# Linear attention and a gated feed-forward layer on one core: the maxima of k pass through a DRAM row instead of a product

## The chip, the core and the metric

One NeuronCore of a Trainium2 chip runs the whole program. Its engines are TensorE (PE, matmuls; PEld is its weight load), VectorE (DVE), ScalarE (ACT), GpSimd (POOL) and SyncE (SP, which here issues every DMA). Each engine works through its own queue in order, and waits on semaphores of the others. The metric is the device time of one execution in microseconds (us); lower is better.

## What is computed

```python
q_s = softmax(q, axis=-1)              # q, k, v: (8 batches, 8 heads, 576, 64)
k_s = k - np.max(k, axis=2, keepdims=True)
k_s = np.exp(k_s)
k_s = k_s / (np.sum(k_s, axis=2, keepdims=True) + 1e-09)
kv  = np.einsum('bhsd,bhse->bhde', k_s, v)
x   = np.einsum('bhsd,bhde->bhse', q_s, kv)      # as (4608, 512): tokens x (head, dim)
xn  = x / sqrt(mean(x * x, axis=-1) + 1e-06) * rms_g
g, val = xn @ w_gate, xn @ w_val                 # (4608, 1536) each
out = (silu(g) * val) @ w_out                    # (4608, 512)
```

The weights come as 64-bit floats and are turned into 32-bit ones on the chip. The factor for the maximum of k differs for each head and each of its 64 columns, and cancels out of the quotient; it keeps the exponentials in range.

## The kernel before

**Tiles.** Heads go in pairs g = 0..3, so that a pair fills 128 partitions (2 heads x 64 columns). The 4608 tokens are cut into nine blocks j of 512, and d_ff = 1536 into twelve slices of 128; a step s = 12 j + i is slice i of block j, 108 in all. `f1(s, a)` (L839) is the first product for the gate (a = 0) or the value (a = 1), `f2(s)` (L878) the second. To keep accuracy on a faster format each 32-bit operand is split into a rounded high part and the rest (`w_hi`/`w_lo`, `o_hi`/`o_lo`, `h_hi`/`h_lo`), and three passes of four 128x512 matmuls replace one product: a block of 12 matmuls. In the first four steps `f2` is native instead: it multiplies the unsplit 32-bit tiles `gs` and `w`, which the profile shows as 8 matmul records.

**The k chain.** For batch b and pair g: `k_load` brings k in as 116 partitions x 2 heads x 5 rows x 64; `k_max` (L461, DVE) takes the maximum over the five rows, `k_tr` (L486, PE) transposes the result, `k_top` (L491, DVE) reduces it to one maximum for each of the 128 columns, a 128x1 tile `kx`. To subtract it the 128 numbers must lie along the free axis, the same on all partitions: `k_diag` (L333, ACT) puts them on a diagonal and `k_rows` (L500, PE) multiplies ones with that diagonal, which leaves the row on every partition in PSUM. `k_sub` (L506, DVE) subtracts it, `k_exp` (L510, ACT) follows, and `k_mm` (L518, PE) forms k'v and the sums in 20 small matmuls; `kv_hi`/`kv_lo` normalise. From batch 2 on `k_seg(m)` puts the products of three neighbouring pairs into one PSUM tile: `k_mm` of pair m-2, `k_rows` of pair m-1, `k_tr` of pair m. There are 24 such pairs.

**What sets the order.** `ORDER` is a list of some 2,800 step names, written by a planner, in which a suffix (:A, :D, :P) names the engine of a step that may run on several. The program is emitted in that order, so every engine's queue is the list cut down to its own steps. SP issues the DMAs in the list's order too, and stops at one whose buffer isn't free yet. The two PSUM tiles of `f1` (`ps_gv`) are freed by `g_mul` (L844) and `h_mul` (L851) on DVE. At the beginning, `conv_*` steps turn the weights into 32-bit numbers on ACT, DVE and POOL; the attention of blocks 0 and 1 has forms of its own (names with a 0). `n_sum`, `n_t`, `n_y0`, `n_y1`, `n_rows` (L767, L772 to L794) compute a block's root mean square, without which the block's first `g_mul` can't run.

Of the kernel before, what the change touches and what calls it, by code (L numbers as in the profile page):

```python
# [42 lines left out]
f1.0.1.1.2 f1.0.1.1.3 q_sum0.1.0 f1.0.0.2.0 f1.0.0.2.1 f1.0.0.2.2 w_hi.1.0.2:A n_y1.0 f1.0.0.2.3 f1.0.1.2.0 f1.0.1.2.1
f1.0.1.2.2 conv_low.1.2.1 w_lo.1.0:P f1.0.1.2.3 conv_low.3.0.2 conv_sign.0.2 w_lo.1.1:P n_rows.0 k_tr.1.0
conv_low.3.2.1 k_top.1.0 g_mul.0 conv_add.0.2.1 k_diag.1.0:A k_rows.1.0 n_cols.0 f1.1.0 silu.0 q_eps0.1.0 load_w.4.0
k_sub.1.0 load_w.4.1 v_ones.1.1 q_rec0.1.0 load_w.4.2 k_max.1.1 q_mul0.1.0:P conv_mul.2.0 v_load.1.1 conv_mul.2.1
h_mul.0 k_exp.1.0 conv_shift.2.0 f1.1.1 conv_shift.2.1 q_load0.1.3 conv_sign.2.0 conv_low.2.2.1 conv_sign.2.1
# [10 lines left out]
conv_sign.5.0 w_lo.4.1:P x_sq.1.0 x_lo.1.0 conv_mul.5.1 f1.4.0 conv_add.5.2.1 q_sum0.1.2 o_hi.4:A h_mul.3 conv_mul.6.0
o_lo.4:P conv_shift.5.1 conv_low.6.0.2 conv_shift.6.0 o_hi.5:A q_eps0.1.1 f1.4.1 conv_sign.5.1 conv_low.7.2.1 o_lo.5:P
q_rec0.1.1 g_mul.4 conv_mul.6.1 conv_sign.6.0 silu.4 q_mul0.1.1:P conv_shift.6.1 k_tr.1.1 conv_add.5.0.2 f2.3  # L60
q_load.2.0 k_top.1.1 conv_sign.6.1 k_diag.1.1:A conv_low.6.2.1 h_mul.4 conv_mul.6.2 h_hi.4:A conv_add.6.0.2
conv_shift.6.2 w_hi.5.0.2:A conv_sign.6.2 k_rows.1.1 warm.2.13 conv_low.8.0.2 load_w.10.0 k_sub.1.1 q_t0.1.1
load_w.10.1 k_max.1.3 load_w.10.2 w_lo.5.0:P f1.5.0 k_exp.1.1 q_c0.1.1:D w_lo.5.1:P q_max.2.0 w_hi.6.0.2:A q_half.2.0
h_lo.4:P k_mm.1.1 conv_mul.7.0 g_mul.5 f2.4 k_load.2.1 w_lo.6.0:P q_exp.1.3 k_eps.1.1 conv_shift.7.0 silu.5 k_rec.1.1
conv_sign.7.0 conv_add.6.2.1 kv_norm0.1.1:D q_sum0.1.3 conv_mul.7.1 f1.6.0 w_lo.6.1:P conv_mul.7.2 conv_shift.7.1
o_hi.6:A v_ones.1.3 q_eps0.1.2 conv_sign.7.1 v_load.1.3 conv_low.10.0.2 o_lo.6:P q_rec0.1.2 conv_shift.7.2 q_x0.1.1
conv_low.8.2.1 g_mul.6 q_mul0.1.2:P conv_low.10.2.1 conv_sign.7.2 f1.5.1 conv_add.7.0.2 x_hi.1.1:A q_load.2.1 x_sq.1.1
x_lo.1.1 silu.6 conv_mul.8.0 k_tr.1.2 f1.6.1 h_mul.5 x_acc.1.1:P kv_hi.1.1:A w_hi.7.0.2:A k_top.1.2 conv_shift.8.0
conv_add.7.2.1 k_diag.1.2:A h_hi.5:A conv_sign.8.0 kv_hi.1.0:A w_lo.7.0:P conv_mul.8.1 load_w.9.0 k_rows.1.2 h_mul.6
f1.7.0 load_w.9.1 k_sub.1.2 load_w.9.2 h_hi.6:A h_lo.5:P conv_shift.8.1 k_exp.1.2 q_max.2.1 h_lo.6:P conv_sign.8.1  # L70
q_t0.1.2 g_mul.7 w_lo.7.1:P f2.5 conv_mul.8.2 q_c0.1.2:D silu.7 conv_shift.8.2 conv_add.8.0.2 q_half.2.1 conv_mul.9.0
conv_sign.8.2 f1.7.1 o_hi.7:A conv_shift.9.0 conv_add.8.2.1 conv_mul.9.1 conv_sign.9.0 w_hi.8.0.2:A conv_shift.9.1
# [5 lines left out]
conv_mul.11.0 conv_mul.11.1 conv_shift.11.0 conv_add.10.0.2 conv_shift.11.1 f2.8 conv_sign.11.0 conv_sign.11.1
conv_mul.10.2 o_lo.9:P g_mul.9 w_hi.10.0.2:A conv_shift.10.2 silu.9 w_lo.10.0:P k_tr.1.3 f1.9.1 conv_sign.10.2
k_top.1.3 conv_mul.11.2 w_lo.10.1:P k_diag.1.3:A conv_shift.11.2 conv_add.11.0.2 conv_sign.11.2 k_rows.1.3 f1.10.0  # L80
k_sub.1.3 h_mul.9 k_exp.1.3 k_max.2.0 conv_add.10.2.1 f1.10.1 g_mul.10 conv_add.11.2.1 w_hi.11.0.2:A h_hi.9:A
q_eps0.1.3 v_ones.2.0 q_max2.2.0 q_rec0.1.3 w_lo.11.0:P v_load.2.0 o_hi.10:A silu.10 k_mm.1.3 q_mul0.1.3:P f1.11.0
# [857 lines left out]
```

## Time and profile before

| | |
|---|---|
| median of three runs | 1003.16 us (1001.92 to 1003.66) |
| the profiled execution, its own time | 1001.34 us |
| its span in the trace | 999.5 us |
| PE busy | 982.6 us (98%) |
| POOL / ACT / DVE busy | 738.0 / 612.5 / 468.8 us |
| chain that ended last: PE's share | 92% |

The busy time of an engine says how much work it has, not whether anybody waits for it. Matmul records overlap: a 128x512 matmul is recorded with some 0.39 us, while one follows the other every 0.227 us (12 in 2.72 us). So what a product costs is read from the starts of the rows around it, not from its own duration. A wait is shown in brackets behind the row that waited, with the engine and line that ended it.

### The profile page before, as it was taken

The page shows a single profiled execution, that of the slowest core. Times are in us where ns is not written, and L with a number is a line of the kernel's source. Part 1 is how long each engine was busy: PE and PEld are TensorE (multiplying, and loading weights), DVE is VectorE, ACT ScalarE, POOL GpSimd, SP SyncE. Part 2 cuts the span into 40 slices and gives each one's busy share as a digit, 9 for nine tenths or more (in the row PEclk, how much of TensorE's full clock was granted, in tenths as well). Part 3 has the DMA queues.
Part 4 walks back from the last instruction along what each step waited for, and adds up shares of the span by engine and source line. Part 5 has one row for each costly group of instructions (what it writes and reads, how often), then busy time and mean ns, then how long its engine had stood idle before and what let it go on. Part 6 is the DMA issues. An engine that isn't in the chain of part 4 may idle for free.

```text
span 999.5 us, 14416 instructions
## 1 busy us (share of the span) xinstructions
PE 982.6 (98%) x4897; PEld 797.1 (80%) x4897; DVE 468.8 (47%) x1135; ACT 612.5 (61%) x885; POOL 738.0 (74%) x643
## 2 busy tenths in 40 slices
PE   7899999999999999999999999999999999999998
PEld 5567887888888888888888888888888888888886
...
DMA packets 129687, 57.64 MB, mean 58 GB/s; under 512 B 101797, under 2 KB 123597, under 8 KB 129613
## 3 DMA queue, kind: packets, MB, share of 16 engines
...
q14 instruction: 36, 0.29, 0.1%
...
## 4 chain that ended last, share of the span: by engine, by line
PE 92%; DMA 3%; SPq 2%; DVE 2%; issue 0%; ACT 0%; POOL 0%; ACTq 0%; POOLq 0%; DVEq 0%
PE ps_gv L839 57%; PE ps_o L878 29%; PE ps_a L717 2%; PE ps_a L518 2%; DMA raw<-in_moe_w_out_dram 2%; DMA kt<-in_k_dram 1%; PE ps_a L500 1%; SPq L364 1%; DMA qt<-in_q_dram 0%; PE ps_a L646 0%; SPq L600 0%; PE ps_a L767 0%; SPq L450 0%; PE ps_a L486 0%; DVE cm L461 0%
## 5 line engine op out<-in xcount | busy, mean ns | idle before, releaser
L816 POOL TENSOR_TENSOR wl<-w,wh 128x512 fp32r<-128x512 f32 x216 | 278.7, 1297 | 103.9 <-ACT wh L328 102.3
L839 PE MATMUL ps_gv<-xh,wh 128*128 128x512 f32 x864 | 236.5, 395 | 2.9 <-ACT kt L510 1.7
L839 PE MATMUL ps_gv<-xl,wh 128*128 128x512 f32 x864 | 231.3, 390 | 0.0
L839 PE MATMUL ps_gv<-xh,wl 128*128 128x512 f32 x864 | 231.1, 389 | 0.0
L839 PEld LDWEIGHTS ps_gv<-xl,wh 128*128 128x128 f32 x864 | 162.2, 188 | 34.7 <-issue 0.2
L839 PEld LDWEIGHTS ps_gv<-xh,wl 128*128 128x128 f32 x864 | 162.1, 188 | 34.2
L839 PEld LDWEIGHTS ps_gv<-xh,wh 128*128 128x128 f32 x864 | 159.7, 188 | 37.1 <-ACT kt L510 2.1
L848 ACT ACTIVATE gs<-gs 128x512 f32<-128x512 f32 x108 | 68.3, 632 | 164.5 <-DVE gs L844 164.0
L844 DVE TENSOR_TENSOR gs<-ps_gv,r 128x512 f32<-128x512 f32 x108 | 74.1, 686 | 192.1 <-PE ps_gv L839 168.8
L824 POOL TENSOR_TENSOR ol<-w,oh 128x512 fp32r<-128x512 f32 x104 | 135.1, 1299 | 37.7 <-ACT oh L328 37.7
L860 POOL TENSOR_TENSOR hl<-gs,hh 128x512 fp32r<-128x512 f32 x104 | 134.7, 1296 | 29.5 <-ACT hh L328 29.5
L851 DVE TENSOR_TENSOR gs<-ps_gv,gs 128x512 f32<-128x512 f32 x108 | 74.5, 690 | 144.1 <-PE ps_gv L839 123.8
L328 ACT CAST wh<-w 128x1024 fp32r<-128x1024 f32 x108 | 113.1, 1047 | 29.2 <-PE ps_gv L839 28.2
L328 ACT CAST oh<-w 128x512 fp32r<-128x512 f32 x104 | 64.3, 618 | 83.3 <-PE ps_o L878 83.3
L878 PE MATMUL ps_o<-oh,hh 128*128 128x512 f32 x416 | 114.0, 394 | 0.0
L878 PE MATMUL ps_o<-oh,hl 128*128 128x512 f32 x416 | 112.0, 390 | 0.0
L878 PE MATMUL ps_o<-ol,hh 128*128 128x512 f32 x416 | 111.9, 389 | 0.0
L878 PEld LDWEIGHTS ps_o<-oh,hl 128*128 128x128 f32 x416 | 78.1, 188 | 16.7 <-POOL hl L860 0.2
L878 PEld LDWEIGHTS ps_o<-ol,hh 128*128 128x128 f32 x416 | 78.1, 188 | 16.6
L328 ACT CAST hh<-gs 128x512 fp32r<-128x512 f32 x104 | 64.4, 619 | 43.2 <-DVE gs L851 42.0
L878 PEld LDWEIGHTS ps_o<-oh,hh 128*128 128x128 f32 x416 | 76.8, 188 | 15.3 <-issue 0.4
L848 ACT ACT_TABLE_LOAD x43 | 55.2, 1283 | 0.8
...
## 6 DMA issues: line engine op xcount, KB each, us to landing
...
```

Of the source, the lines that this page charges most:

```text
L328: (e.copy if e is nc.scalar else e.tensor_copy)(dst, src)
L364: nc.sync.dma_start(t.rearrange("p (c f) -> p c f", c=NKT), src)
L518: nc.tensor.matmul(ps[h * D:(h + 1) * D, :D + 1], lhsT=ke[:n, h, j], rhs=vt[:n, j, h], start=(j == 0), stop=(j == len(rows) - 1))
L717: nc.tensor.matmul(px[:, c0:c1], lhsT=wt, rhs=mv[:, c0:c1], start=(i == 0), stop=(i == 2))
L816: on(nc.gpsimd).tensor_tensor(out=wl[:, a], in0=W(s % NF, a), in1=wh[:, a].bitcast(F32), op=ALU.subtract)
L824: on(nc.vector).tensor_tensor(out=ol, in0=W(s % NF, 2), in1=wo_[s][0].bitcast(F32), op=ALU.subtract)
L839: nc.tensor.matmul(pd[s], lhsT=m[:, a, c * P:(c + 1) * P], rhs=X[j, c][x], start=(n == 1), stop=(n == 3 * NKT))
L844: nc.vector.tensor_tensor(out=gs, in0=g_[s], in1=r_[s // NF], op=ALU.mult)
L848: nc.scalar.activation(g_[s], g_[s], AF.Silu)
L851: nc.vector.tensor_tensor(out=g_[s], in0=v_[s], in1=g_[s], op=ALU.mult)
L860: on(nc.gpsimd).tensor_tensor(out=hl, in0=g_[s], in1=h_[s][0].bitcast(F32), op=ALU.subtract)
L878: nc.tensor.matmul(po[t], lhsT=a[:, t * P:(t + 1) * P], rhs=w, start=(i == 0 and n == 0), stop=(i == NF - 1 and n == len(terms) - 1))
```

## The change

From batch 2 on `k_diag` and `k_rows` are gone. Two new steps on SP take their place: `k_put` writes the 128x1 tile of maxima to 128 numbers in DRAM, and `k_get` reads them back as one row for each of 116 partitions. `k_sub` reads that row from SBUF; 21 of its 24 runs go to POOL, which can't read PSUM and so couldn't do them before. The pool tag `cm` has three buffers instead of two, and `k_get` takes one of them. Steps 2 and 3 have split second products like those that follow, so two native ones (steps 0 and 1) are left. The order is planned anew from the first instruction on, with a late landing of the new DMAs: 45 steps of the first stretch move from POOL to DVE, 19 from ACT to DVE, and the loads at the beginning stand in another order.

```diff
+    dram = ctx.enter_context(tc.tile_pool(name="dram", bufs=4, space=bass.MemoryType.DRAM))
...
-        cm = ap.tile([P, P], F32, name="cm")[:KP if b else P0].rearrange("p (h d) -> p h d", h=2)
+        cm = ap.tile([P, P], F32, name="cm", bufs=3)[:KP if b else P0].rearrange("p (h d) -> p h d", h=2)
...
         if m >= 2:
             k_mm(*at(m - 2), t)
-        if 0 < m <= NG * (B - 2):
-            k_rows(*at(m - 1), t)
         if m < NG * (B - 2):
-            k_tr(*at(m), t[:, 2 * P:])
+            k_tr(*at(m), t[:, P:])
...
+    def k_put(b, g):
+        row_[b, g] = dram.tile([P, 1], F32, name="row")
+        nc.sync.dma_start(row_[b, g], kx_[b, g])
+
+    def k_get(b, g):
+        mb = ap.tile([P, P], F32, name="cm", bufs=3)[:KP]
+        nc.sync.dma_start(mb, row_[b, g].rearrange("p o -> o p").broadcast_to([KP, P]))
+        mb_[b, g] = mb.rearrange("p (h d) -> p h d", h=2)
...
-silu.60 q_lo.6.1:P k_seg.18 h_mul.60 w_hi.62.0.2:A h_hi.60:A f2.59 w_lo.62.0:P k_eps.6.0 k_load.6.3 k_top.6.2
-k_rec.6.0 k_diag.6.2:A k_sub.6.1 kv_hi.6.0:A h_lo.60:P k_exp.6.1 kv_lo.6.0 w_lo.62.1:P q_x.6.0 store.4.0:A f1.61.0
```

On PE, one `k_seg` in the middle of the program. Before, between two blocks, it has `k_mm` (L518), `k_rows` (L500) and `k_tr` (L486):

```order
L878 MATMUL ps_o<-oh,hl 128x512 x4
L518 MATMUL ps_a<-vt,kt 64x65 x10
L500 MATMUL ps_a<-cm,ones 116x128
L486 MATMUL ps_a<-ident,cm 128x116
L839 MATMUL ps_gv<-xh,wh 128x512 x4
```

Now (L849 and L888 are `f1` and `f2`, L528 is `k_mm`, L487 `k_tr`):

```order
L849 MATMUL ps_gv<-xh,wl 128x512 x4
L528 MATMUL ps_a<-vt,kt 64x65 x10
L487 MATMUL ps_a<-ident,cm 128x116
L888 MATMUL ps_o<-oh,hh 128x512 x4
L888 MATMUL ps_o<-ol,hh 128x512 x4
```

The product with ones has left the queue; what stands on either side is the same kind of block as before.

On DVE, the end of the root mean square of block 1, with `n_rows` (`r`), and the first `g_mul` that needs it. Before, `k_max` (L461) and `k_sub` (L506) stand between the two:

```order
L491 TENSOR_REDUCE kx<-ps_a 128x1
L794 STREAM_TRANSPOSE r<-y 128x512
L461 TENSOR_REDUCE cm<-kt 116x128
L506 TENSOR_TENSOR kt<-kt,ps_a 116x640
L688 RECIPROCAL sm<-sm 128x16
L844 TENSOR_TENSOR gs<-ps_gv,r 128x512
L801 TENSOR_REDUCE yt<-y 32x4 x4
```

Now (L804 is `n_rows`, L854 `g_mul`, L464 `k_max`, L861 `h_mul`):

```order
L676 TENSOR_TENSOR st<-st,sw 128x16
L804 STREAM_TRANSPOSE r<-y 128x512
L854 TENSOR_TENSOR gs<-ps_gv,r 128x512
L668 TENSOR_REDUCE sw<-sm 32x16 x4
L464 TENSOR_REDUCE cm<-kt 116x128
L861 TENSOR_TENSOR gs<-ps_gv,gs 128x512
```

`g_mul` stands right behind `n_rows`, and `k_max` behind `g_mul`; `k_sub` has gone further down. On PE three blocks (both `f1` of step 12 and `f2` of step 11) stand between `n_sum` of that block and the `f1` that needs this `g_mul`, where it was two and a `k_seg`.

On SP, one turn in the middle of the program. Before, the loads of k (`kt`), v (`vt`) and q (`qt`) and the stores (`out_dram`):

```order
L425 DMA kt<-in_k_dram 112x2x320
L425 DMA kt<-in_k_dram 3x2x320
L426 DMA kt<-in_k_dram 1x10x64
L450 DMA vt<-in_v_dram 112x5x64 x2
L450 DMA vt<-in_v_dram 3x5x64 x2
L452 DMA vt<-in_v_dram 1x2x64
L586 DMA qt<-in_q_dram 32x12x32 x4
L586 DMA qt<-in_q_dram 32x4x32 x4
```

Now `k_put` (L496) stands between the loads of k and v, and `k_get` (L500) behind the load of q:

```order
L496 DMA row<-kx 128x1
L453 DMA vt<-in_v_dram 112x5x64 x2
L453 DMA vt<-in_v_dram 3x5x64 x2
L455 DMA vt<-in_v_dram 1x2x64
L906 DMA out_dram<-ot 128x512 x2
L596 DMA qt<-in_q_dram 32x12x32 x4
L596 DMA qt<-in_q_dram 32x4x32 x4
L500 DMA cm<-row 116x128
```

From batch 4 on the list has three blocks of PE between a pair's `k_put` and its `k_get`, three or four between `k_get` and `k_sub`, and eleven or twelve more up to its `k_mm`. In batches 2 and 3 it is closer: for pair 2 of batch 2 `k_get`, `k_sub` and `k_mm` stand with one block between the first and the last.

## Rows read from the trace of the kernel before

**Rows 1.** The profile's page: busy time, share and instructions of each engine.

```profile
PE 982.6 (98%) x4897; PEld 797.1 (80%) x4897; DVE 468.8 (47%) x1135; ACT 612.5 (61%) x885; POOL 738.0 (74%) x643
```

**Rows 2.** Three of six stretches of the span. Columns: the stretch (us), its length, then busy time and, in brackets, instructions of PE, PEld, DVE, ACT and POOL, the granted clock of TensorE (1.00 is all of it), the DMA engines' share, GB/s.

```profile
30.00:63.00 33.00, 28.17 (x120) 18.36 (x119) 27.71 (x58) 27.34 (x36) 22.42 (x17) 1.00 0.80 243
63.00:175.00 112.00, 110.09 (x549) 85.78 (x546) 80.99 (x170) 92.80 (x140) 105.65 (x87) 1.00 0.47 134
...
275.00:725.00 450.00, 450.00 (x2318) 371.61 (x2317) 210.04 (x543) 287.69 (x411) 332.91 (x287) 1.00 0.19 44
```

**Rows 3.** The waits of PE over the whole span: the line that waited, what ended the wait, us in total, times, longest. The rows left out are waits in the first 33 us.

```profile
PE ps_gv L839 <- ACT kt L510: 1.7, 1, 1.7
PE ps_a L500 <- ACT cm L333: 1.7, 1, 1.7
...
PE ps_a L518 <- DVE w L385: 1.3, 1, 1.3
PE ps_gv L839 <- DVE gs L851: 1.2, 1, 1.2
...
PE ps_a L486 <- DVE y L790: 0.4, 1, 0.4
```

**Rows 4.** The timeline of PE around one `k_seg` with all three parts. Columns, here and in the other timelines: start, duration, engine, line, operation, tiles, shapes, number of records in the row, and in brackets a wait ahead of it.

```profile
311.15 1.07 PE L878 MATMUL ps_o<-oh,hl 128*128 128x512 f32 x4
...
312.89 0.47 PE L500 MATMUL ps_a<-cm,ones 128*116 128x128 f32 x2
313.20 0.26 PE L486 MATMUL ps_a<-ident,cm 116*128 116x116 f32 x1
...
314.24 1.08 PE L839 MATMUL ps_gv<-xl,wh 128*128 128x512 f32 x4
```

**Rows 5.** The timeline of PE around the `k_seg` without a transpose (739 to 742), and around the one that is `k_mm` alone (763 to 766).

```profile
739.12 1.07 PE L878 MATMUL ps_o<-oh,hl 128*128 128x512 f32 x4
...
740.85 0.47 PE L500 MATMUL ps_a<-cm,ones 128*116 128x128 f32 x2
...
742.09 1.07 PE L839 MATMUL ps_gv<-xl,wh 128*128 128x512 f32 x4
...
763.03 1.07 PE L839 MATMUL ps_gv<-xh,wl 128*128 128x512 f32 x4
...
765.80 0.39 PE L878 MATMUL ps_o<-ol,hh 128*128 128x512 f32 x1
```

**Rows 6.** The timeline of PE around a `k_rows` that stands alone between two groups of matmuls of `f1`.

```profile
128.76 1.08 PE L839 MATMUL ps_gv<-xh,wl 128*128 128x512 f32 x4
129.68 0.38 PE L500 MATMUL ps_a<-cm,ones 128*116 128x128 f32 x2
...
130.83 0.39 PE L839 MATMUL ps_gv<-xl,wh 128*128 128x512 f32 x1
```

**Rows 7.** The timeline of PE around a native `f2` (8 records), and further on around a split one (12).

```profile
48.06 3.59 PE L878 MATMUL ps_o<-w,gs 128*128 128x512 f32 x8
51.49 0.60 PE L633 MATMUL ps_a<-ident,xl 128*128 128x128 f32 x4
...
755.78 1.07 PE L878 MATMUL ps_o<-oh,hh 128*128 128x512 f32 x4
...
758.50 1.07 PE L839 MATMUL ps_gv<-xh,wh 128*128 128x512 f32 x4
```

**Rows 8.** The timeline of DVE at the end of the root mean square of block 1, and the row of PE that waits there.

```profile
156.24 0.70 DVE L794 STREAM_TRANSPOSE r<-y 128x512 f32<-128x512 f32 x1
156.87 1.28 DVE L461 TENSOR_REDUCE cm<-kt 116x128 f32<-116x640 f32 x1
...
158.96 0.62 DVE L844 TENSOR_TENSOR gs<-ps_gv,r 128x512 f32<-128x512 f32 x1
...
159.73 1.17 PE L839 MATMUL ps_gv<-xh,wh 128*128 128x512 f32 x4 [1.72 <-ACT kt L510]
```

**Rows 9.** The timeline of ACT ahead of the diagonal of the first pair of batch 1, and the `k_rows` of PE that waits for it.

```profile
39.70 0.68 ACT L371 ACTIVATE w<-w 128x512 int32<-128x512 uint32 x1 [0.43 <-DMA w<-in_moe_w_out_dram]
40.28 0.39 ACT L333 ACTIVATE cm<-ident,kx 128x128 f32<-128x128 f32 x1
...
40.72 0.48 PE L500 MATMUL ps_a<-cm,ones 128*116 128x128 f32 x2 [1.67 <-ACT cm L333]
```

**Rows 10.** The timelines of SP and DVE: the eight DMAs of one `q_load` and the last one of a `k_load`, then the `q_max` and the `k_max` that wait for them.

```profile
318.99 3.78 SPq L586 DMA_DIRECT2D qt<-in_q_dram  x8
...
337.68 0.68 SPq L426 DMA_DIRECT2D kt<-in_k_dram  x1
...
324.46 0.69 DVE L652 TENSOR_REDUCE st<-qt 128x16 f32<-128x512 f32 x1 [3.74 <-DMA qt<-in_q_dram]
...
340.11 1.32 DVE L461 TENSOR_REDUCE cm<-kt 116x128 f32<-116x640 f32 x1 [0.29 <-DMA kt<-in_k_dram]
```

**Rows 11.** Groups of instructions by line with their shapes: busy time and mean ns of one | idle time ahead of them. L816 is `w_lo`, L669 `q_sub`, L510 `k_exp`.

```profile
L816 POOL TENSOR_TENSOR wl<-w,wh 128x512 fp32r<-128x512 f32 x216 | 278.7, 1297 | 103.9 <-ACT wh L328 102.3 <-PE ps_a L767 1.6
...
L669 POOL TENSOR_TENSOR qt<-qt,st 128x512 f32<-128x512 f32 x28 | 29.4, 1053 | 18.5 <-DVE st L666 15.6 <-issue 2.2 <-POOL ol L824 0.3
...
L510 ACT ACTIVATE kt<-kt 116x640 f32<-116x640 f32 x28 | 20.7, 740 | 4.6 <-DVE kt L506 4.2
```

More of the change, by code (lines that the diff above doesn't have):

```diff
@@ L43 @@
[L43 to L47, printed above, removed]
@@ L58 @@
[L58 to L62, printed above, removed]
@@ L63 @@
[L63 to L72, printed above, removed]
@@ L78 @@
[L78 to L82, printed above, removed]
@@ new lines @@
+conv_add.10.0.2 o_hi.9:A v_load.2.0 h_lo.8:P load_w.11.0 k_rows.1.3 kv_hi.1.0:A w_hi.10.0.2:A conv_add.10.2.1
+w_lo.10.0:P q_t0.1.3 o_lo.9:P w_lo.10.1:P q_half.2.1 k_sub.1.3 load_w.11.1 q_load.2.2 load_w.11.2 x_acc.1.2:P
+conv_mul.11.0 k_max.2.0 k_exp.1.3 q_c0.1.3:D f2.8 h_mul.9 conv_shift.11.0 conv_mul.11.1 f1.10.0 conv_sign.11.0
+conv_shift.11.1 k_mm.1.3 conv_sign.11.1 g_mul.10 h_hi.9:A h_lo.9:D q_max.2.2 o_hi.10:A conv_low.11.0.2 conv_low.11.2.1
+conv_add.11.0.2 f1.10.1 k_eps.1.3 q_sub.2.0:P silu.10 q_half.2.2 k_rec.1.3 kv_norm0.1.3:A k_seg.0 k_top.2.0 h_mul.10
@@ new lines @@
+n_sum.2 q_max.3.3 silu.22 x_hi.2.3:A k_exp.3.0 k_put.3.1 x_lo.2.3 o_lo.20:D q_mul.3.1:D q_half.3.3 f1.23.0 o_hi.21:A
+h_hi.21:A h_mul.22 f1.23.1 k_seg.6 h_lo.20:P o_lo.21:P g_mul.23 n_t.2 f2.20 h_lo.21:P w_hi.24.0.2:A n_y0.2 n_y1.2
+w_hi.25.0.2:A w_lo.25.0:P q_rec.3.2 w_lo.24.1:P q_t.3.1 n_rows.2 k_eps.3.0 w_lo.24.0:P q_max2.3.3 k_get.3.1 v_ones.3.2
+q_sub.3.3:P f1.24.0 silu.23 h_hi.22:A q_hi.3.0:A h_mul.23 q_load.4.0 g_mul.24 k_rec.3.0 q_lo.3.0:P h_lo.22:P
+kv_hi.3.0:D k_top.3.2 f1.25.0 q_max.4.0 f2.21 f1.24.1 o_hi.22:A q_exp.3.3 o_lo.22:P q_mul.3.2:P k_sub.3.1:P k_load.3.3
@@ new lines @@
+x_lo.4.0 o_hi.37:A q_hi.4.2:A o_lo.37:P f1.37.1 g_mul.37 q_load.5.1 k_max.4.3 q_lo.4.2:P silu.37 f1.38.0 h_mul.37
+w_hi.39.0.2:A h_hi.37:A w_lo.39.0:P k_get.4.2 store.2.2:A h_lo.37:P f1.38.1 g_mul.38 store.2.3:A w_lo.39.1:P silu.38
+f2.36 h_mul.38 w_hi.40.0.2:A q_max.5.1 w_lo.40.0:P q_half.5.1 w_lo.40.1:P f1.39.0 o_hi.38:A h_hi.38:A o_lo.38:P
+h_lo.38:P f2.37 g_mul.39 k_sub.4.2:P silu.39 q_max2.5.1 k_exp.4.2 q_sub.5.1:P k_seg.11 f1.39.1 k_eps.4.1 k_load.5.0
+v_ones.4.3 k_top.4.3 o_hi.39:A k_rec.4.1 kv_hi.4.1:A o_lo.39:P q_exp.5.1 k_put.4.3 kv_lo.4.1 v_load.4.3 q_sum.5.1
@@ new lines @@
+k_sub.5.3:P q_exp.6.2 f2.52 h_mul.53 h_hi.53:A q_sum.6.2 w_hi.55.0.2:A h_lo.53:P q_half2.6.2 k_seg.16 k_exp.5.3
+w_lo.55.0:P o_hi.54:A f1.54.0 k_eps.5.2 k_load.6.1 k_top.6.0 k_rec.5.2 w_lo.55.1:P kv_hi.5.2:A kv_lo.5.2 k_put.6.0
+o_lo.54:P q_x.5.2 g_mul.54 v_ones.6.0 q_sum2.6.2 v_load.6.0 silu.54 f1.54.1 q_t.6.0 q_rec.6.2 q_mul.6.2:P x_hi.5.2:A
+q_load.6.3 x_sq.5.2 x_lo.5.2 f2.53 w_hi.56.0.2:A x_acc.5.2:P h_mul.54 k_max.6.1 h_hi.54:A w_lo.56.0:P f1.55.0
+o_hi.55:A h_lo.54:P k_get.6.0 w_lo.56.1:P o_lo.55:P f1.55.1 g_mul.55 silu.55 f2.54 h_mul.55 w_hi.57.0.2:A q_max.6.3
@@ new lines @@
+f1.63.0 o_hi.62:A h_hi.62:A o_lo.62:P h_lo.62:P f2.61 g_mul.63 k_sub.6.2:P silu.63 q_max2.7.1 k_exp.6.2 q_sub.7.1:P
+k_seg.19 f1.63.1 k_eps.6.1 k_load.7.0 v_ones.6.3 k_top.6.3 o_hi.63:A k_rec.6.1 kv_hi.6.1:A o_lo.63:P q_exp.7.1
+k_put.6.3 kv_lo.6.1 v_load.6.3 q_sum.7.1 q_x.6.1 w_hi.65.0.2:A h_mul.63 q_half2.7.1 f2.62 x_hi.6.1:A w_lo.65.0:P
+q_t.6.3 x_sq.6.1 x_lo.6.1 h_hi.63:A q_load.7.2 x_acc.6.1:P q_hi.6.3:A f1.64.0 h_lo.63:P o_hi.64:A k_max.7.0
+w_lo.65.1:P o_lo.64:P f1.64.1 g_mul.64 silu.64 q_lo.6.3:P k_get.6.3 q_sum2.7.1 q_rec.7.1 f2.63 h_mul.64 w_hi.66.0.2:A
```

468 lines of the change are left out of this document (236 added, 232 removed).

## The prediction

> **What bounds the kernel now.** I read the page's shares first, then the span cut into stretches, then PE's waits, then the timelines where PE waits or works off the products that go. The shares say PE 98%, POOL 74% [rows 1], an average over unlike stretches. The stretches settle it: from 275 to 725 us PE is busy for 450.00 of 450 us, and from 63 to 175 for 110.09 of 112; only from 30 to 63 us is it short, 28.17 of 33 [rows 2]. The granted clock is 1.00 in all of them, so no time is to be had from it. After 33 us PE waits in five places only: 0.4, 1.7, 1.2 and 1.3 us before 63 us, and 1.7 us later [rows 3]. So the time is a head of some 63 us, set by loads and by the conversion of the weights, and behind it the plain sum of PE's work. What leaves PE's queue behind the head shortens the run in full, as long as no other engine comes late.
>
> **The product with ones.** What it costs is read from the starts around it. A block of 12 matmuls takes 2.72 us (755.78 to 758.50) [rows 7], 0.227 us each. Around a full `k_seg` the starts run from 311.15 to 314.24 [rows 4]: 3.09 us, less eight matmuls of 0.227 (1.81) leaves 1.28 us. Without a transpose it is 742.09 - 739.12 - 1.81 = 1.16, and for `k_mm` alone 765.80 - 763.03 - 1.81 = 0.96 [rows 5]. So the transpose costs 0.12 and the product 0.20; the sum of a record's 0.47 us [rows 4] would be too much, since records overlap. A product that stands alone costs 130.83 - 128.76 - 1.81 = 0.26 [rows 6]. The 24 that go stand in `k_seg`s, so I take 0.20: 24 x 0.20 = 4.8 us, and 24 x 0.26 = 6.2 as the bound. No less than 4.8, for PE has no idle time there that could swallow it [rows 2].
>
> **The second products.** A native one takes 51.49 - 48.06 = 3.43 us, a split one 2.72 [rows 7]. Two are changed: 2 x 0.71 = 1.4 us less on PE. It adds four casts on ACT, three subtractions on POOL at 1.30 [rows 11] and one on DVE, between 63 and 90 us. POOL, which does 105.65 us of work in 112 there [rows 2], would have no room for 3.9 us more; what makes room is the list, which takes 45 steps off POOL in the first stretch. I count them at nothing. If that cover were missing, PE would wait up to 3.9 us.
>
> **The wait at 158 us.** `n_rows` ends at 156.94, but `g_mul` starts at 158.96, since `k_max` and `k_sub` stand between them on DVE; the next `f1` has no free PSUM tile and starts at 159.73, after 1.72 us [rows 8]. The label names ACT's `k_exp`; I put it down to `g_mul`, because the `f1` that starts there writes the tile that `g_mul` read, and both end within 0.1 us. In the new list `g_mul` follows `n_rows` at once, and three blocks of PE (8.2 us) instead of two cover the chain. I take all of it as gone: 1.7 us; bounds 0 and 1.7.
>
> **The head.** The waits of 0.4, 1.7, 1.2 and 1.3 us [rows 3] sum to 4.6 us. The largest shows their kind: the diagonal is at 40.28 behind a conversion that waited for its load until 39.70, and `k_rows` starts at 40.72 [rows 9]. The new list puts that `k_rows` amid the matmuls of step 0, and has all loads, conversions and `f1` pieces of the head in another order, so each of the four places is gone as such; but the amount of work up to each step is nearly the same, and new places will come. The trace can't show them. Bounds: all 4.6 gone, or 4.6 more. I take half as gained, 2.3, because the late part of the old waits came from ACT working off conversions in an unlucky order, not from a lack of bytes.
>
> **The DMAs that come in.** Every DMA here is issued by SP. Eight of a `q_load` take 3.78 us to issue, and `q_max` runs 1.69 us after the last (322.77 to 324.46); a `k_load` ends its issue at 338.36 and `k_max` runs at 340.11, 1.75 us later [rows 10]. So `k_put` and `k_get` take about 0.68 + 1.75 each, 4.9 us for the trip. From batch 4 on the list leaves 8.2 us (three blocks) from one to the other, as much again to `k_sub`, and some 30 us to `k_mm`. SP spends 48 x 0.68 = 33 us more on issuing, which delays nobody. Behind a waiting `k_put` stand the loads of v, stores and a load of q; `k_put` waits for `k_top`, which follows the `k_seg` that also frees v's buffer, so it holds them back by little, and v is used two `k_seg`s later. Behind `k_get` stands the next load of k. Cost: 0.
>
> **k_sub on POOL** has no row. A broadcast operand costs 1.053 us for 512 columns, two full ones 1.297 [rows 11]; for 640 columns that is 1.32 to 1.62. I take 1.6, two full reads being nearer. 21 of them are 34 us, against 45 steps at 1.0 to 1.3 that leave POOL. Late in the program only the addition remains: about 17 x 1.6 = 27 us on top of 332.91 in 450 [rows 2], 80%. That hides behind PE. The Trainium skill speaks against it: GPSIMD Engine Reference, section Key points, says that GpSimd shares its SBUF interfaces with VectorE and contends with DVE instructions that have two SBUF inputs, which the moved `w_lo`, `h_lo` and `o_lo` on DVE now are. No row here shows that pair at work; if contention doubled all 21, POOL would be at 86% there, still hidden. ACT loses 24 diagonals, which nobody waits for.
>
> **Sum.** From the profiled execution's 1001.34 us: -4.8 -1.4 -1.7 -2.3 = -10.2, so 991.1. The median of the runs stands 1.82 higher, at 1003.16; on that scale **993.0**.
>
> **Rivals.** *The head gives nothing back* (B): new places wait as long as the old ones did, the 1.7 us included. For it: the same bytes and conversions must come first, and DVE's share grows. Against it: POOL's load up to 175 us falls. Only the products and native steps count: 1003.16 - 6.2 = 997.0.
> *What PE saves is waited off* (D), so that the change doesn't do what it says: the new head has twice the old waits (4.6 + 1.7 = 6.3 us more), by splits that come before POOL is free. 1003.16 - 6.2 + 6.3 = 1003.3, no change.
> *The row comes late* (C), slower: in batches 2 and 3, eight pairs, the list is close. For pair 2 of batch 2 one block (2.7 us) stands between `k_get` and `k_mm`, but issue, landing, `k_sub` and `k_exp` need 0.68 + 1.75 + 1.6 + 0.74 [rows 10, 11] = 4.8, so PE is 2.1 us short unless SP runs ahead of the list, as it may. A POOL that waits in `k_sub` holds up `w_lo` and `h_lo` behind it as well. From six such pairs on (12.6 us) the gain is gone by more than can be measured: 1005.6, and with all eight (16.8) 1009.8; middle 1007.7. For it: SP's queue is in order and also holds stores that wait for PE. Against it: only one or two pairs are that close. The Trainium skill, DMA: Bandwidth & Descriptors, section Specifications, adds a reason: below 512 bytes a transfer does read-modify-write, and `k_put` writes 128 pieces of 4 bytes. No run here shows a write so small; a trip made longer by it would tighten all eight pairs.
>
> **How the numbers follow.** A 0.50 (993.0), B 0.26 (997.0), D 0.12 (1003.3), C 0.12 (1007.7). The low end takes every gain at its bound: 6.2 + 1.4 + 1.7 + 4.6 = 13.9, 989.3, so 989. The high end leaves out C and the upper half of D: 1001.5. A measurement of this kernel can tell some 0.2% (2 us) from no change; faster than 1001.2 is all of A and B, within 1001.2 to 1005.2 is D, above is C: 0.76, 0.12, 0.12.
>
> **What would show it.** A `k_seg` of 1.28 - 0.20 = 1.08 us between its neighbours; PE without waits from 63 us on, none at the first `g_mul` of block 1; the waits between 30 and 63 us summing to some 2 us; `k_sub` on POOL near 1.6 us. I am wrong if PE shows waits at `k_mm` in batches 2 and 3 that end with `k_exp` (C), or if the first `f1` of step 5 comes as late as before or later (B, D). If the product's place still costs time with the product gone, the first term fails.

## The result and the profile after

The changed kernel takes 1012.5 us (median of four runs, 1010.8 to 1013.9) against 1002.5 of the kernel before beside it: ratio 1.0097, 95% interval 1.0079 to 1.0116. It is 10 us slower where the prediction had 10 us less. The profiled execution took 1012.48 us, its span is 1010.7.

The page's shares, to be read against [rows 1]:

```profile
PE 981.8 (97%) x4857; PEld 797.4 (79%) x4857; DVE 516.7 (51%) x1178; ACT 564.5 (56%) x825; POOL 728.2 (72%) x622
```

PE's busy time is the same as before, within 1 us. That is no sign that the products still cost something: part of the new run goes at half the clock (0.50, rows below), where the same work counts for more. The span cut into stretches shows it (columns as in [rows 2]):

```profile
30.00:63.00 33.00, 32.21 (x140) 22.23 (x140) 30.32 (x64) 31.25 (x44) 28.56 (x27) 1.00 0.89 256
63.00:175.00 112.00, 112.00 (x568) 90.94 (x567) 94.80 (x189) 85.29 (x126) 91.74 (x72) 1.00 0.50 126
175.00:225.00 50.00, 44.46 (x224) 36.14 (x223) 34.88 (x78) 26.99 (x39) 27.79 (x22) 0.93 0.45 51
225.00:275.00 50.00, 47.87 (x240) 38.63 (x239) 41.18 (x94) 24.36 (x33) 29.79 (x24) 0.97 0.16 33
275.00:325.00 50.00, 41.36 (x211) 33.20 (x210) 26.88 (x65) 22.90 (x36) 24.45 (x21) 0.93 0.40 55
...
375.00:725.00 350.00, 349.55 (x1784) 287.33 (x1783) 162.97 (x418) 202.94 (x295) 281.52 (x238) 1.00 0.20 47
```

The head is better than before: 32.21 of 33 us busy against 28.17, then 112.00 of 112 against 110.09 [rows 2]. All is lost between 175 and 325 us, in batches 2 and 3. PE stands idle there for 5.54 + 2.13 + 8.64 = 16.3 us, and the granted clock, 1.00 before, is 0.93, 0.97 and 0.93. It is at its lower level, 0.50 (1.2 of 2.4 GHz), in three places:

```profile
181.95:188.70 6.75, 5.37 (x13) 4.40 (x14) 4.22 (x12) 2.83 (x5) 1.27 (x1) 0.50 0.22 50
229.75:233.10 3.35, 3.35 (x9) 2.57 (x8) 3.21 (x6) 2.11 (x3) 1.24 (x2) 0.50 0.45 112
294.60:301.30 6.70, 3.14 (x7) 2.51 (x8) 1.30 (x4) 0.00 (x0) 2.95 (x3) 0.50 0.90 69
```

PE works there for 5.37 + 3.35 + 3.14 = 11.9 us. At 1.00 that work takes about half as long (four matmuls of `f1` 0.91 us from start to start at 403.72, and 1.70 at 184.14), so the clock costs some 6 us on top of the waits. From 325 us on PE is as good as gap-free.

The waits of PE behind 35 us, the four largest (columns as in [rows 3]):

```profile
PE ps_o L888 <- DVE ot L338: 6.9, 1, 6.9
PE ps_a L727 <- DVE kv_lo L570: 5.7, 2, 5.0
PE ps_gv L849 <- DVE gs L861: 2.5, 3, 1.7
PE ps_a L487 <- DVE cm L464: 1.2, 1, 1.2
```

None is at `k_mm` (L528), where the rival C looked for them. They are at `f2` behind a store's buffer, at `q_x` (L727) behind a load of q, at an `f1`, and at a transpose behind a load of k. DVE is named each time, but DVE had been waiting itself, and the chain of waits says for what. Here it is from 280 to 310 us (start, duration, what):

```profile
280.24 8.44 DMA row<-kx
...
288.73 4.96 DMA cm<-row
...
293.76 8.34 DMA out_dram<-ot
...
302.12 2.00 DMA qt<-in_q_dram
```

One `k_put` is under way for 8.4 us, the `k_get` behind it for 5.0, a store behind the next `k_put` for 8.3, and the load of q only then. SP's own waits from 128 us on name the same thing (us in total, times, longest):

```profile
SPq L596 <- DMA row<-kx: 62.8, 16, 6.6
...
SPq L500 <- DMA row<-kx: 30.3, 4, 8.7
```

L500 is `k_get`, which must wait for its row. L596 is `q_load`, which has nothing to do with the row. It waits because the semaphores of SP's DMAs are used in turn, eight of them, so that each DMA waits for the one eight places ahead. That stands in the instructions, here at the third `k_put` (the six DMAs left out use semaphores 3 to 7 and 0):

```
L496 DMA row_1927<-kx_1906 128x1 [waits DMAHW2_49,DVE_49]
...
L596 DMA qt_2008<-in_q_dram 32x6x32 [waits DMAHW1_49]
L596 DMA qt_2008<-in_q_dram 32x6x32 [waits DMAHW2_49]
```

The last line needs semaphore 2 again, and so the landing of the `k_put` at the top. The timeline of SP at that place, `k_put` and the 16 DMAs of two loads of q:

```profile
161.74 0.34 SPq L496 DMA_DIRECT2D row<-kx  x1
...
166.75 13.78 SPq L596 DMA_DIRECT2D qt<-in_q_dram  x16
```

Sixteen take 13.78 us to issue, where twice the eight of [rows 10] would be 7.56; PE's first long wait, 5.04 us at 183.33, is for that q.

### The profile page after: what moved, and what is told of

Read it like the earlier page. It is cut to its first block, busy times and chain, and to the rows that moved or that the text cites. A ratio compares the mean times of both kernels' runs of the same rounds, so it can differ in the third digit from the quotient of the medians.

```text
span 1010.7 us, 14306 instructions
## 1 busy us (share of the span) xinstructions
PE 981.8 (97%) x4857; PEld 797.4 (79%) x4857; DVE 516.7 (51%) x1178; ACT 564.5 (56%) x825; POOL 728.2 (72%) x622
## 4 chain that ended last, share of the span: by engine, by line
PE 86%; DMA 7%; DVE 3%; SPq 1%; issue 1%; ACT 1%; POOL 0%; DVEq 0%; POOLq 0%; ACTq 0%
PE ps_gv L849 52%; PE ps_o L888 27%; DMA out_dram<-ot 3%; DMA kt<-in_k_dram 2%; PE ps_a L727 2%; PE ps_a L528 2%; DMA qt<-in_q_dram 1%; DMA row<-kx 1%; PE ps_gv L398 1%; PE ps_a L487 1%; DMA cm<-row 0%; PE ps_a L656 0%; PE ps_a L777 0%; DVE sw L668 0%; DMA w<-in_k_dram 0%
## 5 line engine op out<-in xcount | busy, mean ns | idle before, releaser
L826 POOL TENSOR_TENSOR wl<-w,wh 128x512 fp32r<-128x512 f32 x202 | 263.2, 1310 | 120.9 <-ACT wh L331 111.8
L849 PE MATMUL ps_gv<-xh,wh 128*128 128x512 f32 x864 | 236.8, 395 | 2.8 <-DVE gs L861 2.5
L849 PE MATMUL ps_gv<-xl,wh 128*128 128x512 f32 x864 | 233.8, 392 | 0.0
L849 PE MATMUL ps_gv<-xh,wl 128*128 128x512 f32 x864 | 232.7, 391 | 0.0
L849 PEld LDWEIGHTS ps_gv<-xl,wh 128*128 128x128 f32 x864 | 163.3, 189 | 34.9
L849 PEld LDWEIGHTS ps_gv<-xh,wl 128*128 128x128 f32 x864 | 163.3, 189 | 34.5
L849 PEld LDWEIGHTS ps_gv<-xh,wh 128*128 128x128 f32 x864 | 160.9, 189 | 37.1 <-DVE gs L861 4.0
L854 DVE TENSOR_TENSOR gs<-ps_gv,r 128x512 f32<-128x512 f32 x108 | 74.5, 690 | 188.9 <-PE ps_gv L849 169.5
L870 POOL TENSOR_TENSOR hl<-gs,hh 128x512 fp32r<-128x512 f32 x95 | 124.3, 1308 | 30.7 <-ACT hh L331 22.5
L834 POOL TENSOR_TENSOR ol<-w,oh 128x512 fp32r<-128x512 f32 x99 | 129.3, 1306 | 23.3 <-ACT oh L331 22.6
L861 DVE TENSOR_TENSOR gs<-ps_gv,gs 128x512 f32<-128x512 f32 x108 | 74.4, 689 | 122.9 <-PE ps_gv L849 107.2
L888 PE MATMUL ps_o<-oh,hh 128*128 128x512 f32 x424 | 117.3, 396 | 7.1 <-DVE ot L338 6.9
L888 PE MATMUL ps_o<-ol,hh 128*128 128x512 f32 x424 | 115.0, 392 | 0.0
L888 PE MATMUL ps_o<-oh,hl 128*128 128x512 f32 x424 | 114.4, 391 | 0.0
L888 PEld LDWEIGHTS ps_o<-oh,hh 128*128 128x128 f32 x424 | 79.0, 190 | 24.1 <-DVE ot L338 7.3
L888 PEld LDWEIGHTS ps_o<-ol,hh 128*128 128x128 f32 x424 | 80.2, 189 | 17.0
L888 PEld LDWEIGHTS ps_o<-oh,hl 128*128 128x128 f32 x424 | 80.0, 189 | 17.1 <-POOL hl L870 0.2
L701 POOL TENSOR_TENSOR qt<-qt,sm 128x512 f32<-128x512 f32 x26 | 28.0, 1077 | 27.9 <-DVE sm L698 27.1
```

What stands on the lines that cost most here:

```text
L701: on(nc.vector).tensor_tensor(out=qt_[j, g], in0=qt_[j, g], in1=sm_[j, g].unsqueeze(2).broadcast_to([P, M, 32]), op=ALU.mult)
L826: on(nc.gpsimd).tensor_tensor(out=wl[:, a], in0=W(s % NF, a), in1=wh[:, a].bitcast(F32), op=ALU.subtract)
L834: on(nc.vector).tensor_tensor(out=ol, in0=W(s % NF, 2), in1=wo_[s][0].bitcast(F32), op=ALU.subtract)
L849: nc.tensor.matmul(pd[s], lhsT=m[:, a, c * P:(c + 1) * P], rhs=X[j, c][x], start=(n == 1), stop=(n == 3 * NKT))
L854: nc.vector.tensor_tensor(out=gs, in0=g_[s], in1=r_[s // NF], op=ALU.mult)
L861: nc.vector.tensor_tensor(out=g_[s], in0=v_[s], in1=g_[s], op=ALU.mult)
```

## The experiments

Theory 1: `k_put` lands late, and what SP issues behind it comes late with it. Theory 2: the new order of batches 2 and 3 is at fault, whatever carries the maxima. Theory 3: the read by 116 partitions is at fault. All times in one paragraph are of kernels that ran on one chip unless said otherwise; there the kernel before took 1001.8 to 1002.1 us.

**e1_landing: small DMAs alone.** For each form:

```diff
+            f()                                           # one put, or one read of a row
+            nc.vector.tensor_scalar_add(src, src, 0.0)    # waits for its landing
```

> This kernel leaves out the whole computation: it issues one small DMA at a time, four times each, and a DVE instruction that waits for its landing, then fills the output with zeros. Theory 1 (the 128 pieces of 4 bytes are slow to land by themselves): about 8 us from issue to the DVE instruction for the 128 pieces of 4 bytes that lie together, 2 to 2.5 us for 4 pieces of 128 bytes and for one of 512. Rival (k_put is late because the other loads of batches 2 and 3 are in the way): about 2 to 2.5 us for every form, since nothing else is in flight here. Theory 3 (the read is at fault): 4 us or more for the row read by 116 partitions, 2 us for the row read once.

Part of the timeline. L40 is the put of 128 pieces of 4 bytes side by side, L43 the same 64 bytes apart, L49 4 pieces of 128 bytes, L55 32 pieces of 4 bytes; L74 is DVE when the put has landed:

```profile
25.98 0.34 SPq L40 DMA_DIRECT2D a<-src  x1
...
33.09 0.23 DVE L74 TENSOR_SCALAR src<-src 128x128 f32<-128x128 f32 x1 [5.91 <-DMA a<-src]
33.34 0.34 SPq L43 DMA_DIRECT2D a<-src  x1
34.85 0.23 DVE L74 TENSOR_SCALAR src<-src 128x128 f32<-128x128 f32 x1 [1.53 <-DMA a<-src]
...
36.87 0.26 SPq L49 DMA_DIRECT2D a<-src  x1
38.08 0.23 DVE L74 TENSOR_SCALAR src<-src 128x128 f32<-128x128 f32 x1 [1.24 <-DMA a<-src]
...
39.76 0.31 SPq L55 DMA_DIRECT2D a<-src  x1
42.72 0.23 DVE L74 TENSOR_SCALAR src<-src 128x128 f32<-128x128 f32 x1 [3.00 <-DMA a<-src]
```

From issue to landing, 7.1 us side by side (33.09 - 25.98; 7.0 to 7.3 in three rounds, 9.6 for the first DMA of the run), 1.5 us when 64 bytes or 512 bytes apart (1.9 in the last round), 1.2 us as 4 pieces of 128 bytes or one of 512, 3.0 us for 32 pieces of 4 bytes side by side, and 1.4 us for 32 pieces of 16 bytes, which are as many bytes as the first form. So neither the number of pieces nor the bytes make it slow, but pieces of 4 bytes that are neighbours in DRAM: (7.1 - 1.5) / 128 = 44 ns for each, as an estimate, and (3.0 - 1.5) / 32 = 47 for the short form. The row read by 116 partitions took 2.7 us (22.78 to 25.45, with another put issued 0.46 us ahead of it) and the row read once 1.24. The rival falls, since next to nothing else was in flight: a read of 512 bytes, issued 0.27 us ahead of the put. Theory 3's 4 us for the read isn't met.

The slow put's time doesn't pass in the DMA engines' own packets. For 5.5 of its 7.1 us their share and their GB/s (the last two columns) are nil:

```profile
27.50:33.00 5.50, 0.00 (x0) 0.00 (x0) 1.00 0.00 0
```

**e2_fast_put: the maxima leave in 4 pieces of 128 bytes.**

```diff
+        kr = small.tile([P, 32], F32, name="kr")
+        nc.vector.transpose(kr, kx_[b, g].broadcast_to([P, 32]))
...
-        nc.sync.dma_start(row_[b, g], kx_[b, g])
+        nc.sync.dma_start(row_[b, g].rearrange("(a c) o -> a (c o)", c=32),
+                          kr.rearrange("(a r) c -> a r c", r=32)[:, 0])
```

> The kernel after, with one DVE transpose ahead of k_put, so that the maxima leave from 4 partitions as pieces of 128 bytes. Order, list and number of DMAs are the same. Theory 1: k_get no longer stands behind k_put for 8 us, SP's waits on row fall from 93 us to under 20, PE's waits between 175 and 325 us from 16 to under 4, time 990 to 997 us. Theory 2 (the new order of batches 2 and 3 is itself at fault: loads that stand too late in the list, steps moved to DVE): the waits stay, 1008 to 1013. Theory 3 (the read): the same, 1008 to 1013.

989.1 us, ratio 0.9879 (0.9860 to 0.9898): faster than both kernels, with the same list. PE's only wait behind 35 us, and SP's issue of the 16 DMAs that took 13.78 us above (two views):

```profile
PE ps_gv L852 <- DVE gs L864: 1.0, 3, 0.5
```

```profile
169.36 8.07 SPq L599 DMA_DIRECT2D qt<-in_q_dram  x16
```

The transpose costs DVE 0.20 us each. Theories 2 and 3 said 1008 or more, and fall as explanations of the loss.

**e3_fixed_row and e4_no_put: the wait of k_get taken away, then k_put as well.**

```diff
-        nc.sync.dma_start(mb, row_[b, g].rearrange("p o -> o p").broadcast_to([KP, P]))
+        nc.sync.dma_start(mb, fixed.rearrange("p o -> o p").broadcast_to([KP, P]))
```

and in e4 every `k_put` taken off the list.

> The kernel after, in which k_get reads a row of constants written once early, so the maxima are not subtracted but the number 4, which cancels out of the quotient; k_put is still issued, with no reader. So k_get never waits for k_put, but a k_put that lands late still holds up the eighth DMA behind it. Theory 1 with the direct wait as its main part: 990 to 997 us. Theory 1 with the turn of eight as its main part: 1000 to 1009, SP's waits at L596-like loads of q on row stay near 60 us. Theories 2 and 3: 1008 to 1013.

> As the kernel with the fixed row, but k_put is left out altogether; k_get stays, with its read by 116 partitions, the order too. Theory 1: 990 to 996 us, no wait of PE over 1.5 us between 175 and 325 us. Theory 2: 1008 to 1013. Theory 3: 1006 to 1013, since the read is as before.

e3: 1004.3 us, ratio 1.0019 (1.0003 to 1.0036). e4: 987.5 us, ratio 0.9863 (0.9847 to 0.9880). In e3 nobody needs the row, and still SP's loads of q wait for it:

```profile
SPq L632 <- DMA row<-kx: 39.2, 15, 3.7
```

So the price of `k_put` splits in two, by the ratios. From e4 to e3 (1.0019 - 0.9863) it is 15.6 us, for what `k_put` does to the DMAs behind it; from e3 to the changed kernel (1.0097 - 1.0019) 7.8 us, because `k_get` waits for it at the head of SP's queue; each of the two is known to some 2 us. The read with its 116 pieces, which e4 keeps, costs nothing that can be seen: e4 is the fastest of all.

**e5_spread_put: e3 with the pieces 64 bytes apart.**

```diff
-        row_[b, g] = dram.tile([P, 1], F32, name="row")
+        row_[b, g] = dram.tile([P, 16], F32, name="row")[:, :1]
```

> The kernel with the fixed row (it subtracts the number 4 in place of the maxima, and k_put has no reader), with one change: the 128 pieces of 4 bytes of k_put lie 64 bytes apart in DRAM and not side by side. Number, size and place of the pieces in the list stay. Theory 1, sharpened by the landing times alone (7.0 us side by side, 1.5 us when 64 bytes apart): the turn of eight is free again, 987 to 990 us, as without k_put. Rival, after the rule that a transfer under 512 bytes does read-modify-write: pieces of 4 bytes are dear wherever they lie, 1003 to 1006 us, as with the fixed row.

988.75 us, ratio 0.9876 (0.9858 to 0.9894), so the 15.6 us between e3 and e4 are gone although 128 pieces of 4 bytes are still written. It is the neighbourhood of the pieces, in the kernel as alone.

**e6_product_in_2_3: the product back in batches 2 and 3, the slow k_put from batch 4 on.**

```diff
+        if 0 < m <= 2 * NG:
+            k_rows(*at(m - 1), t)
         if m < NG * (B - 2):
-            k_tr(*at(m), t[:, P:])
+            k_tr(*at(m), t[:, 2 * P:])
```

> The kernel after, with the old product in batches 2 and 3 (k_diag behind k_top on ACT, k_rows in k_seg, k_sub on DVE) and the slow k_put from batch 4 on, 16 of 24. Theory 1: from batch 4 on the list has room for a landing of 7 to 8 us, so nothing is lost there, and 8 products cost 8 x 0.20 = 1.6 us more than the version with the fast put (989.1): 990 to 993 us. Theory 2 (the new order of batches 2 and 3 is at fault whatever carries the maxima): 1005 to 1013. If the slow landing costs time in every batch: 996 to 1005.

997.3 us, ratio 0.9957 (0.9942 to 0.9972). By its number this is the third case, but the trace speaks against that case. From the start of `g_mul` of step 28 to that of step 80, e6 takes 756.49 - 297.72 = 458.77 us, e2 with the fast put 458.21, the changed kernel 459.57 and the one before 462.76. So from batch 4 on the slow `k_put` costs 0.6 to 1.4 us in all. What e6 lacks against e2 was lost by step 28, beside 8 products (1.6 to 2 us) in two waits of PE that e2 hasn't, and 0.97 of the clock from 225 to 275 us (1.5):

```profile
PE ps_a L757 <- DVE xl L779: 2.7, 2, 2.5
PE ps_a L757 <- ACT acc L774: 1.9, 1, 1.9
```

The first ends with DVE, which works off a `g_mul`, a `w_lo` and that `xl` in a row; all eight `k_sub` of these batches are on DVE in e6, which may have pushed it there. The second I can't place. So 990 to 993 was too low for a reason of e6's own, and what e6 leaves of theory 2 is at most these two waits and the clock, some 6 us. That the slow `k_put` costs so little from batch 4 on fits the list: from `k_put` to `k_sub` it leaves six or seven blocks there, 16 us or more, and to `k_mm` eight to thirteen more (not the eleven or twelve said above).

**e7_put_by_pool and e12_put_by_act: k_put from other queues.**

```diff
-        nc.sync.dma_start(row_[b, g], kx_[b, g])
+        nc.gpsimd.dma_start(row_[b, g], kx_[b, g])      # e7; e12: nc.scalar
```

> The kernel after, with k_put issued by GpSimd and not by SP, so it has a queue and semaphores of its own and no longer takes a place in the turn of eight. It still lands late, and k_get still waits for it at the head of SP's queue. Theory 1, turn of eight as the larger part (1004.3 - 987.5 = 16.8 us by the fixed row and the kernel without k_put): 1012.5 - 16.8 = 995.7, 992 to 1000 us; SP's waits on row at the loads of q are gone, those at k_get stay at 30 us or more. If the direct wait is what matters: 1005 to 1013. If GpSimd pays more than about 2 us for each issue in batches 2 and 3, some us on top.

> The kernel after, with k_put issued by ACT and not by SP. It keeps its place in the turn of eight semaphores that SP's DMAs also go through, but leaves SP's queue. Reading 1 (the turn of eight alone): as after, 1008 to 1013 us, SP's loads of q wait on row as before. Reading 2 (place in SP's DMA queue): as with GpSimd's put, 992 to 998 us. Both: in between. ACT issues 24 DMAs more, 0.4 us each, and waits for kx there, which costs PE little.

e7: 993.8 us, ratio 0.9926 (0.9908 to 0.9944). e12, on another chip: 997.7 us, ratio 0.9952 (0.9934 to 0.9971); its rows are from the slowest of its four runs, 1002.4 us. SP's waits on the row, first e7, then e12:

```profile
SPq L500 <- DMA row<-kx: 36.4, 3, 15.6
```

```profile
SPq L596 <- DMA row<-kx: 45.6, 11, 7.3
SPq L500 <- DMA row<-kx: 38.6, 4, 17.5
```

With GpSimd's put the loads of q no longer wait on the row, only `k_get` does. With ACT's put SP still takes part in the same turn and waits 45.6 us at loads of q, yet 14.5 us of the loss are gone by the ratios (17.1 in e7; against e4, 8.9 us stay in e12 and 6.3 in e7). So the turn of eight alone, reading 1, doesn't carry the loss. One thing e7 and e12 have in common: SP no longer stands at `k_put` until `kx` is there, as it did for up to 11.1 us, with all loads behind it. By itself that costs nothing: in e5 SP stands there just as long, 19.3 us in three waits, 11.1 at most, as in the changed kernel. So why the two gain is not shown.

**e11_behind_a_put: a load and a store behind one put, nothing else in flight.**

```diff
+                put()                 # none, side by side, 64 bytes apart, 4 pieces, by ACT
+                load()
+                store(t % 36)
```

> This kernel leaves out the whole computation: three times it issues, with nothing else in flight, a load of 112 x 5 x 64 numbers and a store of 128 x 512, first alone, then behind a put of 128 pieces of 4 bytes side by side, behind one with the pieces 64 bytes apart, behind one of 4 pieces of 128 bytes, and behind the side-by-side put when ACT issues it; DVE waits for the load, ACT for the store, GpSimd for the put. Reading 1 (only SP's turn of eight is held up): load and store land as soon behind the slow put as alone, about 2 and 3 us after their issue. Reading 2 (what stands behind a slow put in the same DMA queue lands after it as well): load and store land 5 us or more later behind the side-by-side put, and as if alone behind the other two; with ACT's put as if alone if each engine has a queue of its own, late if the writes hold up the DMA engines or the memory themselves.

Three of the five forms, second round; L38 is the load, L70 DVE when it has landed, L45 the put, L57 ACT's put, L60 GpSimd when the put has landed:

```profile
40.08 0.32 SPq L38 DMA_DIRECT2D kt<-in_k_dram  x1
...
42.43 0.33 DVE L70 TENSOR_SCALAR kt<-kt 128x320 f32<-128x320 f32 x1 [2.37 <-DMA kt<-in_k_dram]
...
43.95 0.34 SPq L45 DMA_DIRECT2D row<-src  x1
44.38 0.38 SPq L38 DMA_DIRECT2D kt<-in_k_dram  x1
...
52.78 0.61 POOL L60 TENSOR_SCALAR src<-src 128x128 f32<-128x128 f32 x1 [14.68 <-DMA row<-src]
52.88 0.37 DVE L70 TENSOR_SCALAR kt<-kt 128x320 f32<-128x320 f32 x1 [8.82 <-DMA kt<-in_k_dram]
...
64.78 0.33 ACTq L57 DMA_DIRECT2D row<-src  x1
64.97 0.32 SPq L38 DMA_DIRECT2D kt<-in_k_dram  x1
...
73.37 0.38 DVE L70 TENSOR_SCALAR kt<-kt 128x320 f32<-128x320 f32 x1 [8.43 <-DMA kt<-in_k_dram]
```

Alone the load lands 2.35 us after its issue, behind the slow put after 8.50 (52.88 - 44.38), 0.1 us behind the put itself; in the third round it is 10.6, 2.2 us behind the put. The store takes 2.6 us alone and 10.5 behind it. Behind the other two forms both are within 0.6 us of alone. Behind ACT's put the load takes 8.4 to 9.6 us, so leaving SP's queue doesn't help what is issued right after. Reading 2 holds, in its stronger form. The Trainium skill has both halves of this: DMA: Bandwidth & Descriptors, section Issuing engines are not separate DMA queues, says that DMAs of all issuing engines run on the same 16 DMA engines, and its section Queues, rings and completion order says that a DMA's semaphore write lands only after every earlier write of that DMA engine, across queues. The rows of ACT's put agree.

**e8_before_no_product: the first term by itself.** The kernel before, its list without `k_diag` from batch 2 on, `k_sub` subtracting 4 there:

```diff
-        if 0 < m <= NG * (B - 2):
-            k_rows(*at(m - 1), t)
```

> The kernel before, in its own order, without k_diag and k_rows from batch 2 on; k_sub subtracts the number 4 from a constant tile in place of the maxima. This is the first term of the prediction by itself. By the working: 24 x 0.20 = 4.8 us less, ratio 0.9952 (997.3 on this scale), 6.2 at most. Rival (the product lies beside other work): no change, 1002.

998.0 us, ratio 0.9963 (0.9951 to 0.9975): 3.8 us less, 2.5 to 4.9. The starts of `g_mul` say more. Against the kernel before, e8 is 2.16 us late at step 14 (168.92, 166.76) and 3.20 early at step 80 (758.29, 761.49): 5.4 us for the 22 products between, 0.24 each, 5.9 for all 24. It came late to step 14 because its clock was down in two stretches where it was 1.00 before:

```profile
40.00:50.00 10.00, 8.85 (x30) 6.69 (x31) 9.93 (x21) 9.87 (x14) 5.68 (x6) 0.83 0.54 128
...
150.00:175.00 25.00, 23.06 (x114) 18.29 (x113) 19.04 (x53) 17.79 (x25) 19.38 (x21) 0.93 0.28 77
```

**e9_fast_put_again and e10_native_f2: the second products.** e10 is e2 without `o_hi`, `o_lo`, `h_hi`, `h_lo` of steps 2 and 3:

```diff
-o_hi.2:A h_hi.2:A o_hi.3:A o_lo.2:P h_lo.2:P o_lo.3:P h_hi.3:A h_lo.3:D
```

> The version with the fast put once more, beside the next kernel on the same chip, as the better version and as the base for the term of the second products. Theory 1: 987 to 991 us, ratio 0.986 to 0.990.

> The version with the fast put, with the second products of steps 2 and 3 native again (no o_hi, o_lo, h_hi, h_lo there), the list otherwise the same. By the term of the prediction 2 x 0.71 = 1.4 us slower than the version with split ones. Rival (the casts and subtractions that the split ones need on ACT, POOL and DVE cost PE more than they save): 1 us or more faster.

e9: 988.3 us, ratio 0.9869 (0.9852 to 0.9885). e10: 990.75 us, ratio 0.9890 (0.9875 to 0.9904). Native is 2.1 us slower by the ratios; the intervals overlap, so the sign fits the term of 1.4 us and the size is not settled.

## Why the prediction was wrong

The starts of `g_mul` in the five traces show where time was won and lost (us; a step is not quite the same work in the old order and the new):

| step | before | after | e2 | e4 | e8 |
|---|---|---|---|---|---|
| 12 | 158.96 | 149.60 | 151.99 | 149.18 | 159.79 |
| 28 | 298.73 | 313.10 | 293.09 | 289.65 | 299.52 |
| 40 | 405.50 | 419.36 | 398.78 | 395.40 | 405.19 |
| 80 | 761.49 | 772.67 | 751.30 | 747.91 | 758.29 |

The changed kernel is as early as e4 at step 12 (0.4 us apart) and 23.5 us later at step 28. PE's 16.3 us of waits and the 6 us of clock make 22.3 of these, so next to nothing else went wrong.

**The step that failed** is the one on the DMAs that come in: "about 0.68 + 1.75 each, 4.9 us for the trip", "which delays nobody", "it holds them back by little", "Cost: 0". The rows it was priced by were loads [rows 10]; a write of 128 neighbouring pieces has no such row. Alone it took 7.1 us and the read 2.7, in the kernel 8.4 and 5.0, so the trip is 9.8 to 13.4 us. And it delays others: a load issued behind it lands after it (8.5 us and not 2.35 in e11), and SP's loads of q wait for it in their turn (62.8 us). The cost was 23.4 us by the ratios of e4 and of the changed kernel (1.0097 - 0.9863), of which 7.8 through `k_get`'s own wait and 15.6 through the DMAs behind.

**Rival C** had the sign and the batches, but not the mechanism. It priced 2.1 us for each pair whose row is late at `k_mm`, 12.6 to 16.8 us. PE never waits at `k_mm`; the bill came through loads of q and k and through stores. That SP's queue is in order and also holds stores was named there as a point for it, and it deserved to be the mechanism. The Trainium skill's rule (DMA: Bandwidth & Descriptors, section Specifications) that a transfer below 512 bytes does read-modify-write pointed at the right instruction, but its condition, size alone, doesn't tell the slow write from the fast ones here: the same 4-byte pieces land in 1.5 us 64 bytes apart, and 128-byte pieces in 1.2 us.

**The products.** 4.8 us, bound 6.2: by e8 it is 5.9. In the trace of after a full `k_seg` reads so:

```profile
408.25 1.07 PE L888 MATMUL ps_o<-oh,hl 128*128 128x512 f32 x4
...
411.08 1.08 PE L849 MATMUL ps_gv<-xl,wh 128*128 128x512 f32 x4
```

411.08 - 408.25 - 1.81 = 1.02 us, where 1.08 was forecast and 1.28 stood before [rows 4]: a product cost 0.26, nearer to the bound (the one that stood alone) than to the 0.20 taken. The term is right, a little small.

**The wait at 158 us** is gone, with no wait of PE between 63 and 175 us. Right.

**The head** was put at 2.3 us, half of its waits. e4 has all of the change but `k_put`. By its ratio it gains 13.7 us; less 5.9 for products, 1.4 for `f2` and 1.7 for the wait that leaves 4.7, give or take 2. Two stretches of e4 show it directly (columns as in [rows 2]):

```profile
0.00:30.00 30.00, 22.49 (x165) 15.00 (x165) 23.11 (x57) 19.26 (x38) 15.04 (x36) 1.00 1.01 238
30.00:63.00 33.00, 32.51 (x142) 22.58 (x143) 30.18 (x64) 31.20 (x43) 28.88 (x28) 1.00 0.91 268
```

From 30 to 63 us PE idles 0.49 us where it was 4.83 [rows 2]; up to 30 us it works 22.49 us where it was 23.67, so 1.2 us of the 4.3 were paid there. The head gave 3 to 5 us: mis-sized, on the side of caution.

**The second products**: the sign stands, 1.4 us lies within what e9 and e10 leave open.

**k_sub on POOL** was taken at 1.6 us, hidden:

```profile
L516 POOL TENSOR_TENSOR kt<-kt,cm 116x640 f32<-116x640 f32 x21 | 33.9, 1614 | 0.0
```

1614 ns, and POOL's `w_lo` went from 1297 ns [rows 11] to 1310. Right. The contention that the Trainium skill warns of (GPSIMD Engine Reference, section Key points) came, and the trace agrees with the page: DVE's `w_lo`, which has two SBUF inputs, takes 0.69 us as a rule (median of 14), and 1.88 beside a `k_sub` on POOL, 0.55 us beyond that one's end:

```profile
264.92 1.58 POOL L516 TENSOR_TENSOR kt<-kt,cm 116x640 f32<-116x640 f32 x1
265.17 1.88 DVE L826 TENSOR_TENSOR wl<-w,wh 128x512 fp32r<-128x512 f32 x1
```

On the whole it stays hidden: the mean of POOL's `w_lo` is 1% longer.

With a put that lands in time, then, the forecast holds: e2's ratio on the old median is 0.9879 x 1003.16 = 991.0 us, where 993.0 was forecast.

**What stays open.** How the 15.6 us divide between the turn of eight semaphores and the late landing of each DMA behind a put: e12 keeps the turn and e11 shows the late landing across queues, but no run has one without the other. Why the put from another queue gains so much (e7, e12), though e11 has the load late behind ACT's put too, stays open with it. Why neighbouring pieces of 4 bytes are slow isn't shown either, only that they are.
